# Three semaphore increments on SyncE after each load of an attention kernel

## The chip, the cores and the metric

The kernel runs on one core of a Trainium2 chip. The core has five instruction streams that run beside each other and meet only through semaphores: TensorE (PE in the profile, with its weight loads as PEld), VectorE (DVE), ScalarE (ACT), GpSimd (POOL) and SyncE (SP). SyncE computes nothing here; it issues the DMAs, which 16 DMA engines carry out. The metric is the device time of one execution in microseconds (us), the median of several runs.

## The reference, cut to what matters

Attention with cached keys and values, and a projection on either side. Inputs are bf16; 8 batches, 112 queries, 640 model columns, 32 heads of 192, 512 keys.

```python
q = (x @ wq)                      # (8,112,640) @ (640, 6144), split into 32 heads of 192
scores = q @ k_cache^T * 192**-0.5   # per batch and head: 112 x 512
p = softmax(scores)
o = p @ v_cache                   # per batch and head: 112 x 192
return o (heads side by side) @ wo   # (8,112,6144) @ (6144, 640)
```

Keys and values are 50 MB each and are read once. With the weights, 117.5 MB come in from HBM.

## The kernel before, in words

The work is cut into 64 **units**. A unit is four heads of one batch; units run through the eight batches of one group of four heads, and then through the next group (`NG` = 8 groups, `NU` = 64 units).

TensorE does, for unit after unit, in the order written at L884 to L894: the scores of unit u (`do_S`, L842, 96 matmuls), the product of probabilities and values of unit u-1 (`do_PV`, L858, 16), a share of the query projection of a later group and of the output projection of an earlier one (`do_Q`, L805, and `do_O`, L823), and the transposes of unit u-1's output (`do_T`, L869). VectorE transposes the keys (`do_KT`, L976: `kr` to `kt`, four pieces a unit, each 128 x 384 words) and works ahead of the scores in `kt`'s three buffers. ScalarE does the exponentials and most copies out of PSUM. GpSimd copies the middle two of the four value blocks into `vm` (`middle`, L1075) and reorders the query weights (`reorder`, L1066).

SyncE is the only engine that issues loads. Its program (L1100 to L1171) first writes down a list `loads`, in a fixed order, and then goes through it: wait until the destination is free, issue, next. Nothing overtakes in this list. The order from the fifth unit on is: the keys of unit u (`load_k`, four loads), the values of unit u-1 (`load_v`, four loads), then up to one load of query weights (`load_wq`) and up to two of output weights (`load_wo`) where they fall due. There are 603 loads: 552 of 196,608 bytes, 48 of 163,840 bytes for `wo`, and three larger ones of `x`. After them come seven stores of the output (L1174).

What a load waits for: keys have three buffers (`NK`), and all four loads of unit u wait for the same thing, the four transposes of unit u-3 (`vKT`, L1132). Values have four (`NV`), and all four loads of unit u wait for the value product of unit u-4 (`pPV`, L1138). So a released buffer sets four loads free at once. Query weights wait for GpSimd's reorder (`gW`), output weights for the output projection (`pO`). Each load adds 16 to its buffer's semaphore when it has landed; the reader (`do_KT` at L972 for the keys, `middle` at L1072 for the values) waits for all four loads, 64.

Of the kernel before, what the change touches and what calls it, by code (L numbers as in the profile page):

```python
# [666 lines left out]
def build_main(nc, x, k_cache, v_cache, wq, wo, out, flag):  # L667
    B, SQ, D = x.shape
    _, H, SK, DH = k_cache.shape
# [10 lines left out]
    NK, NV, NT = 3, 4, 3  # L680
# [2 lines left out]
    RW = DH + 2  # L683
    EARLY = 0
    NM = 2
    PRE = 12
    EARLY_LOADS = ("k1", "q", "v0", "k2", "v1", "k3", "o", "v2")
    QN = (2, 2, 2)
# [3 lines left out]
    items_at = {}  # L692
    unit_of = {it: -1 for it in q_list[:PRE]}
    k = PRE
    for u in range(NU + 1):
        r = (u - 3) % 8
        o = [("O", (u - 3) // 8, r, h) for h in range(2)] if u >= 3 and r < MT else []
        n = QN[u] if u < len(QN) else 2 if u % 2 == 0 else 1
# [6 lines left out]
    items_at[NU] = (items_at[NU][0] + items_at[NU][1], [("O", NG - 1, MT - 1, h) for h in range(2)])  # L705
    order = [("Q",) + it for it in q_list[:PRE]] + [it for u in range(NU + 1) for it in items_at[u][0] + items_at[u][1]]
    pos = {it: n for n, it in enumerate(order)}
# [7 lines left out]
    with ExitStack() as es:  # L715
        def sb(name, shape, dt):
            return es.enter_context(nc.sbuf_tensor(name, shape, dt))

        def sem(name):
            return es.enter_context(nc.semaphore(name))  # L720
# [6 lines left out]
        kr = [sb(f"kr{j}", [128, 16, DH], BF16) for j in range(NK)]  # L727
        vs = [sb(f"vs{j}", [128, 4, VW], BF16) for j in range(NV)]
        vm = [sb(f"vm{j}", [128, 4, MW], BF16) for j in range(NM)]
        kt = [sb(f"kt{j}", [128, 4, 3, 128, 2], BF16) for j in range(NT)]  # L730
# [20 lines left out]
        aX, aEX, aQ, aT, aNM = (sem(n) for n in ("aX", "aEX", "aQ", "aT", "aNM"))  # L751
        vI, vX, vKT, vSM, vRC, vNM, vO, vT = (sem(n) for n in ("vI", "vX", "vKT", "vSM", "vRC", "vNM", "vO", "vT"))
        gI0, gI, gB, gC, gV = (sem(n) for n in ("gI0", "gI", "gB", "gC", "gV"))
        gW, gM = sem("gW"), sem("gM")
        mX = [sem(f"mX{j}") for j in range(3)]
        mK = [sem(f"mK{j}") for j in range(NK)]
        mV = [sem(f"mV{j}") for j in range(NV)]
# [7 lines left out]
        def W(eng, s, v):  # L765
            if v > 0:
                eng.wait_ge(s, v)
# [16 lines left out]
        def _(pe):  # L784
# [42 lines left out]
            def do(it):  # L827
                (do_Q if it[0] == "Q" else do_O)(it)
# [18 lines left out]
            def do_PV(u):  # L847
# [5 lines left out]
                for a in range(4):  # L853
                    for t in range(4):
                        k, e = divmod(a, 2)
                        o0, src, v0 = [(0, vs[u % NV], 31), (1, vm[u % NM], 0), (0, vm[u % NM], DH + 1),
                                       (1, vs[u % NV], 32 + 3 * DH)][t]
# [22 lines left out]
            for m in range(4, MT):  # L880
                do_X(m)
            for it in order[6:PRE]:
                do(it)
# [15 lines left out]
        def _(act):  # L899
# [46 lines left out]
            evac_x(5)  # L946
            for it in order[6:PRE]:
                evac(it)
# [15 lines left out]
        @block.vector  # L964
        def _(dve):
            dve.memset(dmy[:], 0.0)
            dve.memset(pv[:, :, :, RW - 1:RW], 0.0)
            dve.memset(ones[:], 1.0).then_inc(vI, 1)

            def do_KT(u, t):  # L970
                if t == 0:
                    W(dve, mK[u % NK], 64 * (u // NK + 1))  # L972
                    W(dve, pS, 4 * (u - NT + 1))
                src = kr[u % NK][:, t:16:4, :].bitcast(I32).rearrange("p s (c i) -> p c s i", c=3)
                dst = kt[u % NT][:, t].rearrange("p c j e -> p c (j e)").bitcast(I32).rearrange("p c (j s) -> p c s j", s=4)
                dve.transpose(dst, src).then_inc(vKT, 1)  # L976

            def do_NM(u):
                W(dve, pPV, u + 1)
                W(dve, gB, u - 3)  # L980
                dve.tensor_reduce(sm[:].rearrange("p (k e) -> p k e", k=2), pv[0:SQ, :, :, 0:RW:RW - 1],  # L981
                                  axis=mybir.AxisListType.X, op=ALU.add).then_inc(vSM, 1)
                W(dve, vSM, u + 1)
                dve.reciprocal(rinv[:, u % 4, :], sm[:]).then_inc(vRC, 1)  # L984
                W(dve, pT_, u - 1)
                W(dve, vRC, u + 1)
                dve.tensor_tensor(os_[u % 2][:, 0:2 * DH].rearrange("p (e d) -> p e d", e=2), pv[0:SQ, 0, :, 1:1 + DH],  # L987
                                  rinv[:, u % 4, 0:2][:, :, None].broadcast_to([SQ, 2, DH]), op=ALU.mult).then_inc(vNM, 1)

            def do_OE(it):  # L990
                _, g, m, h = it
                n = o_index[it]
                W(dve, pO, n + 1)
                src = ps[:, bank(it), 0:HO]
                cs = slice(HO * h, HO * (h + 1))
                if g == 0:
                    ins = dve.tensor_copy(acc[:, m, cs], src)  # L997
                else:
                    W(dve, vO, n - 2 * MT + 1)
                    ins = dve.tensor_tensor(ob[:, m, cs] if g == NG - 1 else acc[:, m, cs], src, acc[:, m, cs], op=ALU.add)  # L1000
                ins.then_inc(vO, 1)

            def evac_x(m):
                W(dve, pXT, m + 1)
                dve.tensor_copy(xT[:, :, 128 * m:128 * (m + 1)],
                                psb[:, m % 4, 0:D].rearrange("p (c s) -> p c s", c=DC)).then_inc(vX, 1)

            W(dve, gI, 1)
            for m in (0, 2):
                evac_x(m)  # L1010
            for t in range(4):
                do_KT(0, t)
            for m in (4, 6):
                evac_x(m)
            done = 4
            for u in range(NU + 1):
                ahead = 4 * (u + 2) if u < EARLY else 4 * (u + 2) + min(4, u - EARLY + 1)
                todo = list(range(done, min(ahead, 4 * NU)))
                done = max(done, min(ahead, 4 * NU))
                kts = [divmod(n, 4) for n in todo]  # L1020
                oe = [[it for it in half if it[0] == "O"] for half in items_at[u]]
                first = 2 if u >= EARLY else 0
                for it in kts[:first]:
                    do_KT(*it)
                if u > 0:
                    do_NM(u - 1)
                for it in kts[first:3]:
                    do_KT(*it)
                for it in oe[0]:
                    do_OE(it)  # L1030
                for it in kts[3:]:
                    do_KT(*it)
                for it in oe[1]:
                    do_OE(it)
            W(dve, gC, NU + 1)
            dve.tensor_reduce(tot[:], cnt[:], axis=mybir.AxisListType.XY, op=ALU.add).then_inc(vT, 1)
            W(dve, vT, 1)
            dve.tensor_copy(totb[:], tot[:]).then_inc(vT, 1)
            W(dve, pFL, 1)
            dve.tensor_copy(flag[:], ps[0:1, 0, 0:1]).then_inc(vT, 1)  # L1040
            W(dve, vT, 3)

        @block.gpsimd
        def _(gp):
# [6 lines left out]
            for j in range(NV):  # L1051
                gp.memset(vs[j][:, :, 31:32], 1.0)
                gp.memset(vs[j][:, :, 32 + 4 * DH:33 + 4 * DH], 1.0)
            for j in range(NM):
                gp.memset(vm[j][:, :, DH:DH + 2], 1.0)
# [15 lines left out]
            def middle(u):  # L1071
                W(gp, mV[u % NV], 64 * (u // NV + 1))  # L1072
                W(gp, pPV, u - NM + 1)
                for h in range(2):
                    ins = gp.tensor_copy(vm[u % NM][:, :, (DH + 2) * h:(DH + 2) * h + DH].bitcast(I32),  # L1075
                                         vs[u % NV][:, :, 32 + DH * (1 + h):32 + DH * (2 + h)].bitcast(I32))
# [7 lines left out]
            for it in at.get(-1, []):  # L1084
                reorder(*it)
            for u in range(1, NM):
                middle(u)
# [13 lines left out]
        def _(sp):  # L1101
            loads = []

            def add(dst, src, s, count, waits):
                loads.append((dst, src, s, count, waits))

            def load_x(j):
                m0, m1 = XM[j]
# [17 lines left out]
            def load_k(u):  # L1126
                g, b = divmod(u, B)
                src = k_cache[b, 4 * g:4 * g + 4].rearrange("a (j s) d -> (a j) (s d)", s=16)
                for h in range(4):
                    cs = slice(4 * DH * h, 4 * DH * (h + 1))  # L1130
                    add(kr[u % NK][:].rearrange("p s d -> p (s d)")[:, cs], src[:, cs], mK[u % NK], 64 * (u // NK + 1),
                        [(vKT, 4 * (u - NK + 1))])  # L1132

            def load_v(u):
# [20 lines left out]
            for u in range(4, NU + 1):  # L1155
# [4 lines left out]
                for g in range(2, NG):  # L1160
                    d = u - max(4, unit_of[(g - 3, 5, 1)] + 6 if g >= 3 else 0)
                    if 0 <= d < DC:
                        load_wq(g, d)
                for g in range(1, NG):
                    d = u - (8 * g - 1)
                    if 0 <= d < 3:
                        load_wo(g, d)
            for dst, src, s, count, waits in loads:
                for ws, wv in waits:
                    W(sp, ws, wv)  # L1170
                sp.dma_start(dst, src).then_inc(s, 16)  # L1171
            for m in range(MT):
                W(sp, vO, 2 * (MT * (NG - 1) + m + 1))
                sp.dma_start(out.rearrange("b s d -> (b s) d")[128 * m:128 * (m + 1)], ob[:, m, :]).then_inc(mOUT[m], 16)  # L1174
# [48 lines left out]
```

## Time and profile before

| | |
|---|---|
| median of five runs | 431.79 us (429.39 to 435.47) |
| the profiled execution, its own time | 430.98 us |
| span of the profile | 429.3 us |
| TensorE matmul busy | 392.8 us, 92% |
| VectorE, ScalarE, GpSimd busy | 297.3, 261.7, 136.6 us |
| DMA | 120.14 MB, mean 280 GB/s, 84.9% of the 16 engines' span on SyncE's queue |
| keys: issue to landing of one load, median | 3.9 us |
| values: the same | 3.7 us |

How to read it: a line of the profile names the engine, the line of the source and the tile that is written and read. DMA-issuing instructions are not counted as busy; SyncE's appear as "SPq". "issue" as a reason for a wait is time in which an engine waited for nothing that the profile shows. The DMA share is the mean busy share of 16 engines. TensorE is busy for 92% of the span; the rest of the span is what any change around it can win without making its own work less.

### The profile page before, as it was taken

The numbers are of one execution on the slowest core, as the hardware profiler recorded it, in microseconds if no ns is written. First come the engines' busy times: TensorE is split into PE (matmuls) and PEld (weight loads), VectorE is DVE, ScalarE is ACT, GpSimd is POOL, SyncE is SP. The second block draws the span as 40 slices with busy tenths as digits, with TensorE's granted clock in tenths as the row PEclk, the third lists the DMA queues.
The fourth block names the chain that finished last, engine by engine and source line by source line (L and its number), as shares of the span: only waits on it lengthen the run. The fifth ranks groups of instructions, "written<-read, shape, count | busy, mean of one in ns | idle before, by whom it ended". The sixth has DMA issues, their size and how long they took to land.

```text
span 429.3 us, 20938 instructions
## 1 busy us (share of the span) xinstructions
PE 392.8 (92%) x8948; PEld 297.9 (69%) x8948; DVE 297.3 (69%) x570; ACT 261.7 (61%) x549; POOL 136.6 (32%) x410
## 2 busy tenths in 40 slices
PE   7979998888999998899999869999998999989992
PEld 6557776666777776677787647777766777767771
DVE  1649877675887876578777746788767787787741
ACT  3567655555667764576666536667665776665650
POOL 1234444241344423243333412244312332232320
PEclk9999999999999999999999998999999999998998
DMA  8999999988989998789999977889987899898311
GB/s 283 375 369 351 330 327 339 362 268 277 305 279 301 326 322 281 234 276 298 339 317 288 323 242 218 261 256 287 321 294 221 260 310 312 286 292 267 122 33 38
DMA packets 88453, 120.14 MB, mean 280 GB/s; under 512 B 9760, under 2 KB 88352, under 8 KB 88352
## 3 DMA queue, kind: packets, MB, share of 16 engines
q1 hardware_dynamic: 88352, 118.72, 84.9%
q8 instruction: 72, 1.18, 1.1%
q14 instruction: 29, 0.24, 0.2%
HBM read 117.54 MB, written 1.15 MB: 276 GB/s over the span
## 4 chain that ended last, share of the span: by engine, by line
PE 79%; DMA 5%; issue 5%; DVE 4%; SPq 3%; POOL 1%; ACT 0%; DVEq 0%; POOLq 0%
PE ps L858 21%; PE ps L823 18%; PE ps L842 18%; PE ps L805 17%; PE ps L869 4%; DMA kr<-in_k_cache_dram 4%; SPq L1171 3%; DMA vs<-in_v_cache_dram 2%; DVE os L987 1%; DVE kt L976 1%; POOL wqs L1066 1%; DVE rinv L984 0%; DVE sm L981 0%; POOL vm L1075 0%; DVE acc L997 0%
## 5 line engine op out<-in xcount | busy, mean ns | idle before, releaser
L976 DVE STREAM_TRANSPOSE kt<-kr 128x384 int32<-128x384 int32 x256 | 209.0, 871 | 12.8 <-DMA kr<-in_k_cache_dram 12.8
L922 ACT ACTIVATE pT<-ps 128x448 bf16<-128x448 f32 x256 | 118.6, 548 | 69.8 <-PE ps L842 69.8
L823 PE MATMUL ps<-wos,oT 128*128 128x320 bf16 x672 | 110.1, 300 | 1.6 <-ACT oT L939 0.8
L858 PE MATMUL ps<-vs,pT 128*128 128x193 bf16 x512 | 96.5, 249 | 7.1 <-issue 7.1
L805 PE MATMUL ps<-xT,wqs 128*128 128x448 bf16 x420 | 93.0, 355 | 3.9 <-POOL wqs L1066 2.2
L842 PEld LDWEIGHTS ps<-qT,kt 32*128 32x128 bf16 x6144 | 77.7, 93 | 22.9 <-issue 22.0
L842 PE MATMUL ps<-qT,kt 32*128 32x112 bf16 x6144 | 88.8, 209 | 4.3 <-issue 4.2
L858 PE MATMUL ps<-vm,pT 128*128 128x193 bf16 x512 | 85.8, 249 | 3.8 <-issue 3.8
L1092 POOL TENSOR_SCALAR bad<-rinv 112x4 f32<-112x4 f32 x64 | 14.7, 229 | 227.1 <-DVE rinv L984 226.6
L823 PEld LDWEIGHTS ps<-wos,oT 128*128 128x128 bf16 x672 | 63.0, 98 | 28.7 <-issue 1.9
L914 ACT ACTIVATE qT<-ps 128x448 bf16<-128x448 f32 x96 | 52.3, 545 | 35.0 <-PE ps L805 28.1
L981 DVE TENSOR_REDUCE sm<-ps 112x4 f32<-112x8 f32 x64 | 10.6, 166 | 90.0 <-PE ps L858 89.9
L1075 POOL COPY vm<-vs 128x384 int32<-128x384 int32 x128 | 61.2, 509 | 22.1 <-DMA vs<-in_v_cache_dram 16.7
L939 ACT ACTIVATE oT<-ps 128x672 bf16<-128x672 bf16 x64 | 46.7, 730 | 27.4 <-PE ps L869 27.3
L805 PEld LDWEIGHTS ps<-xT,wqs 128*128 128x128 bf16 x420 | 40.4, 98 | 31.0 <-issue 2.9
L929 ACT ACTIVATE os<-ps,rinv 112x192 bf16<-112x192 f32 x128 | 46.9, 418 | 21.3 <-DVE rinv L984 19.6
L858 PEld LDWEIGHTS ps<-vs,pT 128*128 128x128 bf16 x512 | 48.1, 98 | 14.0 <-issue 8.2
L858 PEld LDWEIGHTS ps<-vm,pT 128*128 128x128 bf16 x512 | 47.0, 98 | 4.5 <-issue 4.4
L1000 DVE TENSOR_TENSOR acc<-ps,acc 128x320 f32<-128x320 f32 x84 | 40.9, 486 | 2.8 <-PE ps L823 2.8
L1066 POOL COPY wqs<-wqr 128x384 bf16<-128x384 bf16 x70 | 33.3, 510 | 22.3 <-DMA wqr<-in_wq_dram 22.3
L987 DVE TENSOR_TENSOR os<-ps,rinv 112x384 bf16<-112x384 f32 x64 | 35.7, 558 | 6.5
L869 PE MATMUL ps<-ident,os 112*128 112x112 bf16 x384 | 29.6, 213 | 4.9 <-DVE os L987 4.9
(36 smaller groups left out, 115.5 us busy)
## 6 DMA issues: line engine op xcount, KB each, us to landing
kr<-in_k_cache_dram SPq DMA_DIRECT2D x256, 192.0 KB, 3.9
vs<-in_v_cache_dram SPq DMA_DIRECT2D x256, 192.0 KB, 3.7
wos<-in_wo_dram SPq DMA_DIRECT2D x48, 160.0 KB, 4.2
wqr<-in_wq_dram SPq DMA_DIRECT2D x35, 192.0 KB, 5.2
out_dram<-xs SPq DMA_DIRECT2D x7, 160.0 KB, 2.4
wqs<-in_wq_dram SPq DMA_DIRECT2D x5, 192.0 KB, 4.3
xs<-in_x_dram SPq DMA_DIRECT2D x2, 320.0 KB, 3.4
xs<-in_x_dram SPq DMA_DIRECT2D x1, 480.0 KB, 5.8
```

The source lines that it names most:

```text
L805: mm = pe.matmul(ps[:, bank(it), 0:HQ], wqs[:, g % 2, dc, 128 * c:128 * (c + 1)], rhs, start=(dc == 0), stop=(dc == DC - 1))
L823: mm = pe.matmul(ps[:, bank(it), 0:HO], oT[:, c, 128 * m:128 * (m + 1)], wos[:, g % 2, c, HO * h:HO * (h + 1)], start=(c == 0), stop=(c == 5))
L842: mm = pe.matmul(ps[:, a, SQ * t:SQ * (t + 1)], kt[u % NT][p, t, c // 2, :, c % 2], qT[g % 2][p, c, SQ * b:SQ * (b + 1)], start=(c == 0), ...
L858: mm = pe.matmul(pv[:, k, e, o0:o0 + DH + 1], pT[u % 2][:, a, t, :], src[:, a, v0:v0 + DH + 1], start=(t == 0), stop=(t == 3), skip_group_ ...
L869: mm = pe.transpose(psb[:, 4, o0:o0 + SQ], os_[u % 2][:, 256 * (j // 2) + j % 2:256 * (j // 2) + j % 2 + 255:2], ident[0:SQ, 0:SQ])
L914: act.activation(qT[g % 2][:, c, HQ * h:HQ * (h + 1)], ps[:, bank(it), 0:HQ], ACTF.Copy).then_inc(aQ, 1)
L922: act.activation(pT[u % 2][:, a, :, 0:SQ], ps[:, a, 0:4 * SQ].rearrange("p (t q) -> p t q", t=4), ACTF.Exp, scale=scale).then_inc(aEX, 1)
L929: ins = act.activation(os_[u % 2][:, DH * (2 + e):DH * (3 + e)], pv[0:SQ, 1, e, 1:1 + DH], ACTF.Copy, scale=rinv[:, u % 4, 2 + e:3 + e])
L939: act.activation(oT[:, :, SQ * b:SQ * (b + 1)].rearrange("p (k c) q -> p k c q", k=2), src.rearrange("p k (c q) -> p k c q", c=3), ACTF.Co ...
L976: dve.transpose(dst, src).then_inc(vKT, 1)
L1000: ins = dve.tensor_tensor(ob[:, m, cs] if g == NG - 1 else acc[:, m, cs], src, acc[:, m, cs], op=ALU.add)
L1075: ins = gp.tensor_copy(vm[u % NM][:, :, (DH + 2) * h:(DH + 2) * h + DH].bitcast(I32), vs[u % NV][:, :, 32 + DH * (1 + h):32 + DH * (2 + h) ...
```

## The change

After each load from the 35th on (`FREE = 34`), SyncE increments a new semaphore `sN`, which nobody waits for. A load of 196,608 bytes is followed by three increments, one of 163,840 bytes (`wo`) by two: `NOPS * size // 196608`. The number of pieces of a key buffer gets a name (`KP = 4`), and stays four; the list `loads` carries the size in place of the unused count. No other engine's program changes.

```diff
+    KP = 4
+    NOPS = 3
+    FREE = 34
...
-        gW, gM = sem("gW"), sem("gM")
+        gW, gM, sN = sem("gW"), sem("gM"), sem("sN")
...
-                    W(dve, mK[u % NK], 64 * (u // NK + 1))
+                    W(dve, mK[u % NK], 16 * KP * (u // NK + 1))
...
             def add(dst, src, s, count, waits):
-                loads.append((dst, src, s, count, waits))
+                size = 2
+                for n in dst.shape:
+                    size *= n
+                loads.append((dst, src, s, waits, size))
...
-                for h in range(4):
-                    cs = slice(4 * DH * h, 4 * DH * (h + 1))
-                    add(kr[u % NK][:].rearrange("p s d -> p (s d)")[:, cs], src[:, cs], mK[u % NK], 64 * (u // NK + 1),
+                for h in range(KP):
+                    cs = slice(16 // KP * DH * h, 16 // KP * DH * (h + 1))
+                    add(kr[u % NK][:].rearrange("p s d -> p (s d)")[:, cs], src[:, cs], mK[u % NK], 16 * KP * (u // NK + 1),
                         [(vKT, 4 * (u - NK + 1))])
...
-            for dst, src, s, count, waits in loads:
+            for n, (dst, src, s, waits, size) in enumerate(loads):
                 for ws, wv in waits:
                     W(sp, ws, wv)
                 sp.dma_start(dst, src).then_inc(s, 16)
+                for _ in range(NOPS * size // 196608 if n >= FREE else 0):
+                    sp.sem_inc(sN, 1)
```

## The prediction

> **What bounds the kernel now.** I read the chain that ended last first, then TensorE's waits, then SyncE's.
>
> ```profile
> PE 79%; DMA 5%; issue 5%; DVE 4%; SPq 3%; POOL 1%; ACT 0%; DVEq 0%; POOLq 0%
> ```
>
> The chain is TensorE's own work for 79% of 429.3 us. What could go is in the small shares. Its pieces in order of time show where they lie: all that is DMA, SPq or VectorE stands before 74 us, and from there on the chain is TensorE with "issue" between. So there are two stages: up to about 76 us the loads set the pace, after it TensorE does. TensorE's "issue" waits:
>
> ```profile
> PE ps L858 <- issue: 10.9, 8, 2.1
> ...
> PE ps L842 <- issue: 4.2, 3, 2.0
> ...
> PE ps L805 <- issue: 1.6, 2, 1.3
> ...
> PE ps L823 <- issue: 0.5, 1, 0.5
> ```
>
> Together 17.2 us in 14 stalls. One of them in the order of time:
>
> ```profile
> 89.98 0.33 PE L858 MATMUL ps<-vm,pT 128*128 128x193 bf16 x2
> 91.85 0.33 PE L858 MATMUL ps<-vs,pT 128*128 128x193 bf16 x2 [1.53 <-issue]
> ```
>
> It stops in the middle of sixteen matmuls that wait for nothing. The stalls stand 256 TensorE instructions apart, or a multiple of that, and before nearly each a packet of 16,384 bytes on the instruction queue ended 1.3 to 1.6 us before TensorE went on (here it ran from 89.48 to 90.41 us). So TensorE waits for its own code, fetched by the DMA engines that carry the loads. Now SyncE:
>
> ```profile
> SPq L1171 <- DVE kt L976: 52.5, 98, 1.5
> SPq L1171 <- PE ps L858: 49.6, 39, 3.5
> ```
>
> ```profile
> L1171 SPq DMA_DIRECT2D kr<-in_k_cache_dram x256: 327/430/2008, 4.1 to 391.7; - x128
> ...
> DMA to landing us min/median/max: 2.5/3.9/6.8
> ```
>
> An issue takes 430 ns in the middle, 327 at least, 2008 at most. One by one: loads issued back to back start every 474 ns (430 and a gap of 44). After a gap of 155 ns or more an issue takes 328 (unless it is one of the long ones), and between them length and gap add up to 474 (54 and 425, 71 and 403). So **two issues cannot end less than 474 ns apart, and a gap of up to 146 ns costs nothing**. The long ones (71 above 470 ns) go with instruction packets in many cases; I read them as a full queue. Counted over the loads from 17.7 us on, SyncE is idle for 69.7 us beyond the 45 ns gaps (less than the table's sums, which count a wait from an earlier point) and held in issues above 434 ns for 47.9 us.
>
> **The increments.** 569 loads follow the 34th: 521 with three increments and 48 with two, 1,659 in all. No increment on SyncE is in the trace. The nearest rows: its semaphore instructions take 17 ns (28 with two conditions), and the next instruction starts 65 to 85 ns after their start (72 where a wait that also decrements is followed by a register load). Below, 17 and the shortest gap of 42 make 59; above, 85. I take **72**. Then the gap is 44 + 3 x 72 = 260, more than 146, so the issue takes 328 and loads start every 588 ns instead of 474: +114 (+75 at 59 ns, +153 at 85). With two increments it is 44 + 144 + 328 = 516, +42. Crossing a block of 128 instructions costs SyncE about 0.25 us (loads 77, 205, 333, 461 and 589 start that late); 1,659 instructions add 13 crossings, 3.2 us.
>
> [...]
>
> **Up to 76.5 us.** Between 17.7 and 76.5 us there are 102 loads. SyncE is idle for 0.9 us and held for 9.4. The added 102 x 0.114 = 11.6 us and 0.6 for crossings stand against 10.3 us: +1.9 us, if a later issue means a full queue no longer holds it. It lies on the path, since VectorE starts a unit's transposes 23 ns after its keys landed in units 8 to 10. Bounds: nothing (59 ns: 7.7 us, covered) to +5.9 (85 ns: 15.6 + 0.6 - 10.3).
>
> **From 76.5 us on.** 467 loads, so 467 x 0.114 = 53.2 us, less 2.9 for 40 `wo` loads, and 2.6 for crossings: 52.9 us. Cover: SyncE's idle time, 68.8 us in this stage, and 38.4 us held. It suffices: the wait before a released buffer shrinks by what the increments took. If the cover went, the price would be the uncovered rest; at 474 - 44 - 328 + 0.149 (69 us over 467 loads) the three increments may take 251 ns, 84 each, before the idle time alone is used up, and 111 with the held time. The last of four pieces goes out 3 x 0.114 = 0.34 us later; keys land 3 to 13 us before VectorE takes them from unit 12 on, and values 4 to 13 us before GpSimd does. Hidden: 0.
>
> **What is won.** Bursts of four to eight loads at 474 ns ask for 196,608 B / 474 ns = 415 GB/s:
>
> ```profile
> 20.00:60.00 40.00, 37.50 (x926) 27.92 (x915) 27.72 (x52) 27.34 (x59) 16.48 (x43) 1.00 1.02 351
> ```
>
> Here, at a DMA share of 1.02, they got 351. At 588 ns they ask for 334. What queued up was in front of the code fetches too: I set the request 236 TensorE instructions before its block is needed (the point that no fetch comes ahead of), and from there the packet starts after a median of 1.8 us, with six loads in flight; after 0.2 us at 405 us, with none. That is about 0.3 us a load. A landing without a queue takes 2.5 us; at 588 ns, 2.5 / 0.588 = 4.3 loads are in flight, 1.7 fewer than six, and a fetch comes 0.5 us sooner. Fourteen stalls, each shorter by 0.5: **-7.0 us**. Bounds: 0 (the same bytes go through the same engines) and -17.2.
>
> [...] The row of 1.8 us with loads against 0.2 without speaks for a queue.
>
> **The sum.** 430.98 + 1.9 + 0 - 7.0 = 425.9 us. The profiled run is 0.8 below the median of five, 431.79; I leave that small gap out and predict 425.9, 1.4% under the median. About 1% either way is what a measurement of this kernel tells from no change.
>
> **Rivals.**
> 1. *The fetches don't come sooner.* For: the packet itself takes about 0.95 us and the DMA engines carry 85 to 90% either way. Against: the delay differs by 3 us between quiet and full moments. 430.98 + 1.9 = 432.9. No change.
> 2. *SyncE becomes the bound*: increments wait until the issue before them has let go of the descriptor hardware, so that they add their full 216 ns (690 a load). Against: waits in the gap do overlap (155 ns gaps, 328 ns issues). [...] Up to 76.5 us: 102 x 0.216 + 0.6 - 10.3 = +12.3. After: 467 x 0.216 + 2.6 - 2.9 = 100.6 against 107.2: just covered. With the fetches won, 430.98 + 12.3 - 7.0 = 436.3, slower, and that from 72 ns an increment on (below, the early stage costs less than 4.3 us after the fetches). At 85 ns +16.3 and 467 x 0.255 + 2.6 - 3.4 - 107.2 = +11.1 make 451.4.
> 3. *All fetch stalls go*: 430.98 + 1.9 - 17.2 = 415.7.
> 4. *Nothing moves* since the increments fit into the gap (under 34 ns each): 431. Below the lowest row of 59; counted with rival 1.
>
> **Chances.** The forecast 0.45 (its own range 421 to 430: most of it under 427.5, some within 1%), rival 1 with 4 0.26, rival 2 0.20, rival 3 0.09. The range takes in rival 3 and rival 2 at its row, with 3 to 4 us above it for the early stage at 85 ns (+4.0): 415 to 440; the far end of rival 2 stays out. Faster by over 1%: 0.36 of the forecast and rival 3, 0.45. Within 1%: 0.33, with a little of rival 2. Slower: 0.22, with the early stage at 85 ns.
>
> **What would show it.** On SyncE, issues of 328 ns at a spacing near 588 inside a set of four, and long issues gone; waits for `kt` and L858 down by some 50 us. Landing of keys near 3 us instead of 3.9. TensorE's "issue" waits near 10 us instead of 17.2, at the same places. VectorE's waits for `kr` (12.8 us) up by about 2. Wrong, if the spacing inside a set is near 690 or the waits on SyncE are gone (rival 2), or if issue waits stay at 17 (rival 1). The increment's price and the fetch's place in the queue are what I know least.

## The result, and the profile after

The changed kernel takes 435.77 us in the median (42 runs), the kernel before 431.9 (79 runs). The ratio is 1.0079 with a 95% interval of 1.0056 to 1.0103; like every ratio below it is taken over the runs within 1.5% of their kernel's fastest, while the medians over all runs are 0.9% apart. That is slower by 0.8%, within 1%, and not the 425.9 us that were forecast. The profiled execution took 437.3 us (span 435.6) at a mean granted TensorE clock of 0.981, against 0.988 in the profile before; part of the 6.3 us between the two spans is that clock (TensorE's matmuls are busy for 395.8 us in place of 392.8), so stages are compared below, not spans.

SyncE's issues shrank as the forecast said, but its spacing grew by less, and the long issues stayed. Line L1177 of the changed kernel, SyncE's load issues (shortest, median and longest ns), and the landing of all loads that this line issues:

```profile
L1177 SPq DMA_DIRECT2D kr<-in_k_cache_dram x256: 327/328/1473, 4.1 to 399.8; - x128
...
L1177 SPq DMA_DIRECT2D wos<-in_wo_dram x48: 327/328/1753, 19.6 to 370.0; - x48
...
DMA to landing us min/median/max: 2.3/3.6/6.8
```

The median issue went from 430 to 328 ns. Single records give the rest: the first increment starts 38 ns after the issue ends, the next ones 58 ns apart, the load 72 ns after the last. Loads of a set start every 554 ns; before it was 474, and 588 were forecast. The wide end, 1473 and 1753 ns, is still there: 68 issues took more than 470 ns, 71 before. SyncE's waits, engine line and what it waited for, us in total, times, longest:

```profile
SPq L1177 <- DVE kt L979: 21.3, 58, 1.3
...
SPq L1177 <- PE ps L861: 18.4, 18, 3.0
```

102 us of waiting for released buffers became 40. The increments used up idle time, as foreseen, and in the later stage SyncE still had some (from 17.7 us on 32 us in all, 70 before). TensorE's waits in the changed kernel:

```profile
PE ps L861 <- issue: 12.6, 8, 2.4
PE ps L845 <- issue: 4.6, 3, 2.4
PE ps L808 <- issue: 0.9, 1, 0.9
```

18.1 us in 12 stalls; before, 17.2 in 14. Nothing was won here: the kernels below that change no load's size and take no more than 3% longer have 15.2 to 19.8. The loss shows in busy time by stage (columns: stretch, its length, then busy us and instructions of TensorE, its weight loads, VectorE, ScalarE and GpSimd, the granted clock, the DMA share and GB/s). The kernel before:

```profile
17.70:40.00 22.30, 20.03 (x550) 14.41 (x539) 12.03 (x22) 15.47 (x34) 9.32 (x22) 1.00 1.05 361
40.00:76.50 36.50, 34.97 (x779) 25.87 (x781) 28.04 (x53) 22.23 (x47) 16.52 (x47) 1.00 1.00 335
```

The changed kernel:

```profile
17.70:40.00 22.30, 20.10 (x553) 14.41 (x542) 12.08 (x22) 15.39 (x33) 8.92 (x21) 1.00 1.01 340
40.00:76.50 36.50, 32.30 (x695) 23.79 (x693) 24.67 (x49) 20.60 (x45) 14.81 (x42) 1.00 0.93 299
```

Between 40 and 76.5 us TensorE got through 695 matmuls in place of 779, at the same clock, and the DMA engines moved 299 GB/s in place of 335 and were less busy. VectorE's wait for keys rose, by 5.0 us where about 2 were forecast. Before, and in the changed kernel:

```profile
DVE kt L976 <- DMA kr<-in_k_cache_dram: 12.8, 5, 3.8
...
DVE kt L979 <- DMA kr<-in_k_cache_dram: 17.8, 8, 3.9
```

The chain of the changed kernel:

```profile
PE 80%; issue 6%; DMA 4%; DVE 4%; SPq 2%; POOL 1%; ACT 1%; DVEq 0%; POOLq 0%
```

The "issue" share that was to shrink, 5% before, did not.

### The profile page after: what moved, and what is told of

It is laid out like the page before. It is cut to its first block, busy times and chain, and to the rows that moved or that the text cites. A ratio compares the mean times of both kernels' runs of the same rounds, so it can differ in the third digit from the quotient of the medians.

```text
span 435.6 us, 22597 instructions
## 1 busy us (share of the span) xinstructions
PE 395.8 (91%) x8948; PEld 298.9 (69%) x8948; DVE 297.5 (68%) x570; ACT 261.6 (60%) x549; POOL 136.2 (31%) x410
## 4 chain that ended last, share of the span: by engine, by line
PE 80%; issue 6%; DMA 4%; DVE 4%; SPq 2%; POOL 1%; ACT 1%; DVEq 0%; POOLq 0%
PE ps L861 21%; PE ps L826 19%; PE ps L808 18%; PE ps L845 18%; PE ps L872 4%; DMA kr<-in_k_cache_dram 3%; SPq L1177 2%; DVE os L990 2%; DMA vs<-in_v_cache_dram 2%; DVE kt L979 1%; POOL wqs L1069 1%; DVE rinv L987 1%; DVE sm L984 0%; ACT pT L925 0%; POOL vm L1078 0%
## 5 line engine op out<-in xcount | busy, mean ns | idle before, releaser
L861 PE MATMUL ps<-vs,pT 128*128 128x193 bf16 x512 | 96.9, 250 | 10.3 <-issue 8.4
L808 PE MATMUL ps<-xT,wqs 128*128 128x448 bf16 x420 | 95.3, 362 | 2.8 <-POOL wqs L1069 1.9
L845 PE MATMUL ps<-qT,kt 32*128 32x112 bf16 x6144 | 87.9, 208 | 4.7 <-issue 4.6
L984 DVE TENSOR_REDUCE sm<-ps 112x4 f32<-112x8 f32 x64 | 10.6, 166 | 89.8 <-PE ps L861 89.8
L861 PEld LDWEIGHTS ps<-vs,pT 128*128 128x128 bf16 x512 | 48.1, 98 | 17.2 <-issue 9.5
L990 DVE TENSOR_TENSOR os<-ps,rinv 112x384 bf16<-112x384 f32 x64 | 35.7, 558 | 6.5
L872 PE MATMUL ps<-ident,os 112*128 112x112 bf16 x384 | 29.6, 213 | 5.7 <-DVE os L990 5.6
```

The costliest lines, as they stand in the source:

```text
L808: mm = pe.matmul(ps[:, bank(it), 0:HQ], wqs[:, g % 2, dc, 128 * c:128 * (c + 1)], rhs, start=(dc == 0), stop=(dc == DC - 1))
L845: mm = pe.matmul(ps[:, a, SQ * t:SQ * (t + 1)], kt[u % NT][p, t, c // 2, :, c % 2], qT[g % 2][p, c, SQ * b:SQ * (b + 1)], start=(c == 0), ...
L861: mm = pe.matmul(pv[:, k, e, o0:o0 + DH + 1], pT[u % 2][:, a, t, :], src[:, a, v0:v0 + DH + 1], start=(t == 0), stop=(t == 3), skip_group_ ...
L872: mm = pe.transpose(psb[:, 4, o0:o0 + SQ], os_[u % 2][:, 256 * (j // 2) + j % 2:256 * (j // 2) + j % 2 + 255:2], ident[0:SQ, 0:SQ])
```

## The experiments

**Theory A**: the loss lies in the early stage, in which SyncE has no time to give, and the later stage neither wins nor loses. **Theory B**: the loss comes from the later stage. In a second step, two theories on the long issues and on the code fetches: **Q**, both are a queue behind the bytes of the loads, which pacing would relieve; **F**, a code fetch holds an issue by itself, and is late by itself.

Two stretches are read off single records in each profile: from the scores of unit 3 to those of unit 11 (the early stage, clear of the start, which differs by up to 4 us from one execution to the next whatever the kernel), and from unit 13 to unit 63. Each is one execution: the four kernels without an increment in the early stage lie within 2.5 us of each other there, the two without one in the later stage within 1.7 us.

| kernel | increments early / later | ratio to before (95%) | unit 3 to 11, us | unit 13 to 63, us |
|---|---|---|---|---|
| before | 0 / 0 | | 51.3 | 305.9 |
| e2_late | 0 / 3 | 0.998 (0.994 to 1.002) | 50.3 | 304.3 |
| e8_late2 | 0 / 2 | 1.0005 (0.996 to 1.005) | 52.7 | 307.0 |
| e7_late4 | 0 / 4 | 1.022 (1.016 to 1.027) | 51.1 | 315.5 |
| e1_one | 1 / 1 | 1.005 (1.001 to 1.009) | 53.1 | 308.7 |
| e3_early | 3 / 0 | 1.015 (1.009 to 1.022) | 58.8 | 304.3 |
| changed | 3 / 3 | 1.0079 (1.0056 to 1.0103) | 54.6 | 308.3 |
| e12_changed | 3 / 3 | 1.008 (1.002 to 1.014) | 56.7 | 306.9 |
| e4_six | 6 / 6 | 1.177 (1.169 to 1.186) | 64.5 | 367.4 |

### Increments only later, only early

```diff
-    FREE = 34
+    FREE = 136
```

> Increments only from the load that goes out at about 76.5 us on (FREE = 136). Theory A (the loss lies in the early stage, where loads set the pace, and the increments of the later stage cost and win nothing): ratio to before 0.997 to 1.004, scores of unit 13 within 1 us of before. Theory B (the loss comes from the later stage: loads spaced out meet more of the code fetches): 1.005 to 1.010, scores of unit 13 as before, the loss after it.

```diff
-                for _ in range(NOPS * size // 196608 if n >= FREE else 0):
+                for _ in range(NOPS * size // 196608 if FREE <= n < 136 else 0):
```

> Increments only after loads 34 to 135, up to about 76.5 us. Theory A: ratio 1.005 to 1.009, scores of unit 13 about 4 us later than before (3.9 in the changed kernel's profile), nothing lost after it. Theory B: 0.998 to 1.003.

Measured: 0.998 and 1.015. Leaving out the 102 early loads takes the whole loss away; they alone bring it. The two windows of 40 to 76.5 us, first `e2_late`:

```profile
40.00:76.50 36.50, 36.32 (x789) 27.36 (x781) 29.54 (x57) 23.77 (x52) 16.87 (x47) 1.00 1.01 342
```

and `e3_early`:

```profile
40.00:76.50 36.50, 33.09 (x738) 25.02 (x726) 23.87 (x47) 21.70 (x47) 14.44 (x40) 1.00 0.91 287
```

342 GB/s without increments there, 287 with them. Theory A holds, B falls. Unit 13 of `e2_late` came 3.5 us later than before, not within 1: 2.6 us of that was there at unit 3, ahead of any increment, so the absolute time was a poor thing to forecast and the stretch is a better one. `e3_early` lost more than was expected (1.005 to 1.009), and more than the changed kernel, which has the same increments there and more besides. The intervals overlap; a gain of the later increments would explain it, but `e2_late`, whose interval takes in 1, does not show one, and neither does the stretch from unit 13 on. That stays open.

### One increment, two, four, six

```diff
-    NOPS = 3
+    NOPS = 1
```

> One increment in place of three. From the changed kernel's single instructions (an increment starts 38 ns after the issue, the next load 72 ns after the increment) the gap is 110 ns, inside the 146 that cost nothing: loads still start every 474 ns, with issues of about 364. Then everything is as before, ratio 0.997 to 1.003. If an increment adds its own time to an issue, the spacing is 530 or more, and theory A gives 1.003 to 1.008.

Measured: loads every 474 ns with issues of 372, as expected; 1.005, just above the expected range. The one increment added nothing to SyncE's spacing: 474 ns with it and without. Why the time is 0.5% up, with an interval that just leaves out 1, is not settled: in its one profile loads 34 to 135 took 62.2 us for 58.6, but kernels without increments there took up to 61.7.

```diff
-    NOPS = 3
-    FREE = 34
+    NOPS = 2
+    FREE = 136
```

> Two increments, from the load at 76.5 us on. Spacing 38 + 58 + 72 + 328 = 496 ns, hardly above 474. SyncE's idle time covers it (10 of 69 us). If what three increments there gave (ratio 0.998) is no gain, this is 0.996 to 1.004 too; if spacing wins, it lies between three increments and none.

```diff
-    NOPS = 3
-    FREE = 34
+    NOPS = 4
+    FREE = 136
```

> Four increments, from the load at 76.5 us on. Spacing 38 + 3 x 58 + 72 + 328 = 612 ns. With what the changed kernel showed (issues over 328 ns 35 us and 0.35 us a block of 128 instructions) a group of eight units takes SyncE 69 x 0.612 + 6 x 0.554 + 5.7 + 1.0 = 52.3 us, against 49.7 that TensorE takes: SyncE falls behind by 2.6 us a group over six groups, less the 5 us that keys lie ready: ratio 1.01 to 1.03. If pacing in the later stage wins through fewer bursts, as much as three do or more: 0.993 to 1.000.

Measured: 1.0005 at a spacing of 496 ns, 1.022 at 613. With `e2_late` at 554 (0.998) the later stage has room up to somewhere between 554 and 613 ns, and no gain on the way there. In `e7_late4` keys lie ready for 0.02 to 0.65 us in 23 of the 40 units from unit 24 on; in `e2_late` they lie ready for 1 to 10 us in 37 of them.

```diff
-    NOPS = 3
+    NOPS = 6
```

> Six increments in place of three. Spacing 38 + 5 x 58 + 72 + 328 = 728 ns. A group of eight units then takes SyncE 69 x 0.728 + 6 x 0.612 + 1 = 54.9 us, against 47.2 of work on TensorE plus some 2 of stalls: SyncE is the bound. The last load goes out near 17.7 + 521 x 0.728 + 48 x 0.612 + 6 = 432 us, and with landing, GpSimd's copy and what follows (about 19 us) the time is 445 to 455, ratio 1.03 to 1.055. A price per increment that is hidden further would give less than 1.02.

Measured: 508.8 us, 1.177, far above the expected 445 to 455. Spacing was right (730 ns). The sum had left out that long issues do not go away (35 us above 434 ns), and fell short by some 2 us for the crossings (26 more, at 0.3 us) and by 3 us for a fifth increment behind `wo` loads. With these, 432 becomes 472; the last load went out at 481.7. And with SyncE late all the time a second limit closes, a loop over the key buffers. VectorE's waits in `e4_six`:

```profile
DVE kt L979 <- DMA kr<-in_k_cache_dram: 148.8, 58, 5.6
```

and the engines' shares of its chain:

```profile
DMA 28%; PE 25%; DVE 20%; issue 14%; SPq 8%; ACT 1%; POOL 1%; DVEq 0%; ACTq 0%; POOLq 0%
```

Keys land, VectorE transposes them, that frees the buffer, SyncE issues the next; TensorE is no more than a quarter of it. TensorE's issue waits did fall here, to 9.9 us in 9 stalls: with 3.9 loads in flight (issued and not yet landed) a fetch started a median of 1.17 us after the forecast's mark, for 1.85 before. But TensorE also waited 52.9 us for VectorE (L872 for `os` of L990), so how much of this is pacing is not separated.

### Half the bytes

These two kernels leave out half of the keys from the fourth unit on, and half of the values from the fifth; all instructions stay.

```diff
-                    cs = slice(4 * DH * h, 4 * DH * (h + 1))
+                    cs = slice(4 * DH * h, 4 * DH * h + (4 if u < NK else 2) * DH)
...
-                    add(vs[u % NV][:, a, 32:32 + 4 * DH], v_cache[b, 4 * g + a].rearrange("(m t) d -> m (t d)", t=4),
+                    n = (4 if u < NV else 2) * DH
+                    add(vs[u % NV][:, a, 32:32 + n], v_cache[b, 4 * g + a].rearrange("(m t) d -> m (t d)", t=4)[:, 0:n],
```

> The kernel before, but from the fourth unit of keys and the fifth of values on each of their loads brings only the first half of its columns (98,304 bytes for 196,608); the rest of the buffer keeps older data. The number of loads, their order and their waits stay, and so does everything on the other engines. Theory Q (the long issues on SyncE and TensorE's code waits are a queue behind the bytes of the loads): long issues above 470 ns fall from 71 to under 20, TensorE's issue waits from 17.2 to under 4 us. Theory F (a code fetch holds SyncE's issue, and is late, by itself): 50 to 75 long issues, issue waits above 10 us. On the early stage: if the bytes set its pace (102 loads in 58.6 us, 340 GB/s), loads 34 to 135 go out in under 54 us; if SyncE's spacing of 474 ns and the held issues do, in 56 to 60.

The same halving in the changed kernel, with three increments behind the halved loads:

> The changed kernel with the same halved loads and three increments after each. If SyncE's own time sets the early stage, loads 34 to 135 take 6 to 8 us longer than in the halved kernel without increments (72 ns a load, as in the changed kernel against before: 66.1 against 58.6 us), whole loads or half. If the increments only cost because paced loads leave the DMA engines bytes behind, the difference is under 2 us.

Measured: 421.0 (two runs) and 428.1 us, ratios 0.976 (0.967 to 0.984) and 0.990 (0.985 to 0.995). The DMA queue of the halved kernel without increments:

```profile
q1 hardware_dynamic: 88352, 71.15, 61.8%
```

71 MB and 62% of the engines' time, for 119 MB and 85%. Yet SyncE had 64 issues above 470 ns, for 71 before. Their time above 328 ns, with the early and the later loads added, is 58.4 us, for 54.9. **The long issues are no queue behind bytes.** Against the records of the DMA packets: 61 of the 64 (66 of 71 before, 67 of 68 in the changed kernel) overlap a code fetch within 0.3 us, where 29% of all issues do, and in the median a long issue ends 0.37 us after the packet of a fetch did. The moment hardly varies: where the packet was one of TensorE's (60 of the 71 before), the middle half of the long issues ended 364 to 373 ns after it. Theory F, for the issues.

TensorE's own waits did shrink in `e5_half`:

```profile
PE ps L858 <- issue: 6.6, 7, 1.5
PE ps L842 <- issue: 3.3, 2, 1.8
PE ps L805 <- issue: 0.4, 1, 0.4
```

10.3 us in 10 stalls for 17.2 in 14, and 9.7 us in 9 in `e6_half_paced`. So a fetch does come sooner when there are far fewer bytes in flight: landing took 2.5 us in the median for 3.8, and the packet started 1.27 us after the forecast's mark for 1.85. That lies between the theories: half the bytes won 6.9 us of stalls, and the larger part remained.

The early stage, by what SyncE's 102 loads from the 35th on took:

| | loads 34 to 135, us | issue, ns a load | between issues, ns a load |
|---|---|---|---|
| before | 58.6 | 522 | 53 |
| e2_late | 58.4 | 505 | 68 |
| e8_late2 | 60.8 | 524 | 72 |
| e7_late4 | 61.7 | 517 | 88 |
| e1_one | 62.2 | 485 | 125 |
| changed | 66.1 | 415 | 232 |
| e12_changed | 68.5 | 439 | 232 |
| e3_early | 68.6 | 434 | 239 |
| e5_half | 61.6 | 527 | 77 |
| e6_half_paced | 70.3 | 436 | 253 |

Without increments in this stage whole loads took 58.4 to 61.7 us, with three 66.1 to 68.6. Between the pairs, three increments cost 72 ns a load with whole loads (changed and before) and 85 with half: 7.5 us and 8.7 over this stage. Halving the bytes did not make that less, so the increments are paid in SyncE's own time. `e5_half` took 61.6 us, over the expected 56 to 60, for an idle time and not for issues; that is inside the spread of the kernels with whole loads.

### Fewer and larger loads

If SyncE's time were all that holds the early stage, fewer loads should win.

```diff
-    KP = 4
+    KP = 2
...
-    FREE = 34
+    FREE = 10000
```

> No increments; each key buffer is loaded in two pieces of 393,216 bytes in place of four. The issue of the larger loads of x (327,680 bytes) took 440 ns against 432, so an issue costs the same: SyncE spends 4 x 0.474 + 2 x 0.474 on eight units' worth of pieces where it spent 8. If SyncE's own time sets the early stage (theory A), scores of unit 13 come 1 to 4 us earlier than in the kernel before and the ratio is 0.990 to 0.998. If the bytes set it, 0.998 to 1.004. If larger loads are held longer or land later, above 1.004.

```diff
-                for a in range(4):
-                    add(vs[u % NV][:, a, 32:32 + 4 * DH], v_cache[b, 4 * g + a].rearrange("(m t) d -> m (t d)", t=4),
-                        mV[u % NV], 64 * (u // NV + 1), [(pPV, u - NV + 1)])
+                for a in range(0, 4, 2):
+                    add(vs[u % NV][:, a:a + 2, 32:32 + 4 * DH],
+                        v_cache[b, 4 * g + a:4 * g + a + 2].rearrange("a (m t) d -> m a (t d)", t=4),
+                        mV[u % NV], 32 * (u // NV + 1), [(pPV, u - NV + 1)])
```

> No increments; keys and values of a unit in two loads each. SyncE issues four loads a unit in place of eight. Theory A: ratio 0.985 to 0.997, scores of unit 13 2 to 5 us earlier, until the bytes (20 MB in 58.6 us, at most 375 GB/s: 54) hold it. Rival: the same 0.998 to 1.004.

```diff
-    KP = 4
+    KP = 1
...
-                for a in range(4):
+                for a in range(0, 4, 4):
```

(the values of a unit then in one load, as above with `a:a + 4` and 16 for 64; both have `FREE = 10000`, the first `KP = 2`, and `middle` waits for 32 or 16)

> No increments; keys and values of a unit in one load each of 786,432 bytes. SyncE then has time to spare everywhere. Theory A: no more than with two pieces each, 0.985 to 0.998. If a code fetch queues behind the bytes of an issued load, TensorE's issue waits rise above 17 us and the ratio is over 1.002.

Measured: 1.0095 (1.006 to 1.013), 1.011 (1.005 to 1.018) and 1.011 (1.006 to 1.017). None is faster; over all runs the medians' ratios are 1.006, 1.007 and 1.010. From unit 3 to 11 they took 49.8, 50.1 and 50.3 us, where the four kernels with whole loads and no increments there took 50.3 to 52.7: at most about 1 us was won, though SyncE had far fewer issues to make. Half the bytes took 48.1. Theory A in its strong form, that SyncE's spacing alone sets the early stage of the kernel before, falls; what holds is that SyncE had next to nothing to spare there (0.9 us idle in the kernel before), so that what three increments added was paid. Where larger loads lose is open: from unit 13 to 63 their profiles took 303.4 to 305.0 us, no more than the kernel before. TensorE's issue waits were 17.9, 18.6 and 20.7 us, and a fetch started a median of 2.0 to 2.1 us after the forecast's mark, for 1.85: the sign that the third expectation named for a queue behind the bytes, though a small one.

### The changed kernel once more

No edit; run beside the three kernels with larger loads.

> The changed kernel once more, on the same chip as the three others. Ratio 1.005 to 1.011; loads 34 to 135 in 64 to 68 us, long issues 60 to 75, TensorE's issue waits 15 to 20 us. The early stage's share would show as scores of unit 13 3 to 6 us later than in the kernel before.

Measured: 1.008 (1.002 to 1.014), 66 long issues, unit 3 to 11 in 56.7 us. TensorE's issue waits:

```profile
PE ps L861 <- issue: 14.5, 9, 2.9
PE ps L845 <- issue: 4.4, 2, 2.6
PE ps L808 <- issue: 0.4, 1, 0.4
PE ps L826 <- issue: 0.3, 1, 0.3
```

19.6 us in 13: in a second execution, too, no less than the 17.2 of the kernel before. No kernel of this study beats the one before.

## Why the prediction was wrong

**The increment's price: the working right, the number at its low end.** 72 ns were taken between 59 and 85; the runs show 58 from one increment to the next, 38 ahead of the first and 72 behind the last. The gap of 226 ns was more than the free 146, the issue fell to 328, and the spacing is 554 where 588 was forecast: +80 ns a load, not +114. A gap in which SyncE crosses a block of code is 0.34 to 0.37 us in most cases, about 0.3 more than usual, where 0.25 was taken. Rivals 2 and 4 are out. No run shows increments that wait for the issue before them and add their full 216 ns: the first starts 38 ns after the issue ends, the next issue shrinks from 430 to 328 ns, and the spacing is 554 ns, not 690. Nor do three fit into the free 146 ns: 554 is 80 more than 474.

**From 76.5 us on: right.** Cost 0 was forecast; from unit 13 to 63 the changed kernel took 308.3 and 306.9 us and `e2_late` 304.3, kernels without increments there 305.9 and 304.3, those with one or two 308.7 and 307.0. But the room was less than stated: up to 84 to 111 ns an increment meant a spacing of 623 to 705, and 613 already cost 2.2%. The held time that was counted as reserve was hardly one: the long issues of the later stage kept 33 to 46 us above 328 ns in the kernels with increments and whole loads there, for 44 before.

**Up to 76.5 us: the sign right, the size wrong.** The forecast set 10.3 us of cover against the added 12.2, 0.9 us idle and 9.4 held, on the condition "if a later issue means a full queue no longer holds it". It does not: of 14 long issues 11 remained, and 8.7 of their 10.9 us above 328 ns (11.2 in the second execution, 10.6 in `e3_early`). The holds went with code fetches (67 of the 68 long issues of the changed kernel overlap one), most often with one of TensorE's, and of these every kernel here has 72 packets of 16,384 bytes in its span. The sum also charged all 102 loads with three increments; 12 of them are `wo` loads with two. At the measured prices, 80 ns on 90 loads and 22 on 12, the increments add 7.5 us, and SyncE's stage grew by 7.5 us where 1.9 was the sum, and TensorE's by 3.3 to 7.5 us (54.6, 56.7 and 58.8 against 51.3).

**The code fetches: this step failed.** -7.0 us were forecast from loads in flight falling from six to 4.3, each fetch coming 0.5 us sooner. The loads in flight fell from 5.8 to 5.4 on average at the marks that the forecast used (5.1 in the second execution), and the packets started a median of 1.70 us after the mark (1.54) where it was 1.85: 0.15 to 0.3 us sooner. Loads that go out every 554 ns still land 3.6 us later, not after the 2.5 us that the forecast divided by. The stalls went from 17.2 to 18.1 and 19.6 us. The mechanism is not nothing, since half the bytes took 6.9 us off them; but that is what the forecast gave to pacing. **Rival 1**, the fetches don't come sooner, was the case, and its 432.9 us lacked the part of the early stage that the held time was to cover. That the forecast's range takes in the measured time owes nothing to its own mechanism: the upper end was there for rival 2 and for dearer increments.

Put together by the stretches: about +3 to +5 us in the early stage and nothing clear after it, for +3.9 us between the medians.

## What to carry to other kernels

Idle time is cover only in the stage that has it: SyncE had 70 us to spare in all and 0.9 us in the 59 us where loads set the pace (2.5 to 4.5 in three other kernels without increments there), and there nearly all that the increments added was paid, 72 ns a load. Before a stall is counted as cover, or as something to win, find out what it belongs to; halving the bytes under the same instructions told a queue from a code fetch here (64 long issues for 71). An instruction between two DMA issues took no spacing here as long as it fitted into the time by which the second issue then shrank, 146 ns with the gap that was there: 474 ns with no increment and with one, 496 with two, 554 with three.

## What was not expected of the hardware

- **SyncE's long DMA issues went with code fetches.** In every kernel with loads of 197 KB or less, 92 to 99% of the issues above 470 ns overlapped a code-fetch packet, and in the median they ended 0.37 us after it. 62 to 74 of them cost 34 to 55 us above 434 ns, at 85% DMA load and at 62%. With larger loads fewer overlapped one: 79, 66 and 40%, so there issues were long without one too.
- **Back to back, the issues of the kernel before ended 474 ns apart (never less than 472), and the later one shrank** where something else filled the time: from 430 ns to 372 with one increment between, and to 328 with two or more.
- **SyncE stopped at every 128th of its instructions**: 5 times before and 18 times in the changed kernel, always at the same place in the block. The gap there was 0.34 to 0.37 us but for the first (0.42), where 0.04 to 0.07 is usual. Packets of 8,192 bytes on one instruction queue go with it: 35 before, 48 in the changed kernel, whose 1,659 more instructions are 13 blocks.
- **A lower granted clock went with a longer time.** Over 211 runs with a time and a clock, each kernel with a level of its own, a mean granted TensorE clock lower by 0.01 went with 4.1 us more. The changed kernel's runs had 0.981 in the mean, those of the kernel before 0.983: about 1 us of the difference, and at equal clock the fit leaves 2.9 us. Whether the increments have a hand in the clock stays open.
